# The token gate in one bank and the last group of heads normalised whole

## The chip, the core and the metric

One core of a Trainium2 chip runs the whole program. Its engines work from queues of their own and wait for each other by semaphores: TensorE (PE, matrix products into the eight PSUM banks), VectorE (DVE), ScalarE (ACT), GpSimd (POOL), and SyncE (SP), which here only issues transfers to the 16 DMA engines. The metric is the device time of one execution in microseconds. A profile is one execution taken by the hardware profiler; its span goes from the first to the last instruction.

## The reference

Two attention blocks over the same 2048 tokens of 512 channels, 32 heads of 16, mixed by a gate for each token:

```python
x = A_x
g = _sigmoid((x * gate_w).sum(-1, keepdims=True))
a = _A_ref(x, A_wqkv, A_wo)            # softmax attention
b = _B_ref(x, B_wqkv, B_w_phi, B_wo)   # linear attention with softmax features
return g * a + (1 - g) * b

# _A_ref, a head at a time
p = _softmax((q @ k.T) * Dh ** -0.5)
o = p @ v                              # then all heads @ wo
# _B_ref
phi_q = concat(softmax(q @ w_phi), softmax(-q @ w_phi)); phi_k the same of k
o = (phi_q @ (phi_k.T @ v)) / (phi_q @ sum(phi_k) + 1e-6)
```

Branch A costs most: 32 heads times 2048 x 2048 scores, each of which needs an exponential.

## The kernel before

**Packs.** Branch A is cut into 512 packs. A pack is 4 heads x 128 keys x 512 queries: four score products, one for each 32-row strip of the array (L963), written to four PSUM banks, each 128 x 512. Sixteen packs (all keys) make a group, a set of four heads for one block of 512 queries; there are 32 groups, numbered 0 to 31, eight for each block of queries (`qc`). A pair of groups (even, odd) shares the queries q0 to q15.

**Two ways to an exponential.** ACT takes the scores of most packs in turns of three and two blocks, writing ET (L1011). For the packs that the table `AWAY` names, one entry of five bits for each group, DVE does it instead: `_vector_bits` makes four products and evicts each bank as integers that stand for a power of two (L903, tile va, tag b), and `_vector_terms` adds three shifts to them (L919, tile vp, tag t), two packs at a time where a group has two. The value products (L1077) read ET, va and vp as weights of V (or vc, a scaled copy of V) in four 32-column strips of one bank, adding up a group's numerators and, in a row of ones, its denominators. Where PE would idle, products with zeros (L1084, L984) fill in.

**The plan.** The kernel first makes a list of operations (`Plan.op`), each with an engine, a cost, a due position `prio` counted in packs and an earliest position `rel`. `Plan.order` then simulates the five queues with those costs and takes for each engine the operation that is ready and due first. What comes out is a fixed order for each engine's queue; on the chip each queue runs strictly in that order. `SHIFT` adds an offset in packs to all operations with a tag: p12 is the value product of pack 12, b and t are the bits and terms of DVE packs, x their products, q10 the projection and the transfers of the queries of groups 20 and 21, g the normalisation of a group, gate the gate, n, o, h parts of branch B, y an output block. A PE bank is given to a job when its first product is placed, and given back by the job's last eviction.

**Queries.** `_proj_q` projects the queries of a pair of groups, evicts them (L675, qs) and SP spreads them with eight small transfers to qT (L677). Fifteen lists (q1 to q15) come this way.

**Normalising.** When a group's sums stand, DVE transposes the bank in 32 x 32 blocks into T1 (L1129), multiplies the denominators with 1 + exp(-gate) (L1136, tile gh), takes the reciprocal (L1138) and scales (L1140). For an odd group SP then spreads the pair with 16 small transfers (L1148, tile `turned`) and transposes by DMA into onTA (L1363). The last pair is done by other means, without DMA: group 30 is normalised alone, and group 31 by `_norm_last`, in two halves of 256 columns one after the other, each with transpose (L1107), den (L1111), rec (L1113), mul (L1114) and a transpose back into onTA (L1117).

**Output.** `_out` multiplies onTA with the output weights (L1457), four products `pr` for each tile of 128 tokens, on top of branch B's four (L1411). Of the last block's four tiles (`tt` 0 to 3) the products of the last pair, pr = 3, are the last of all; tt 1 and 3 are evicted by DVE (L1464, with a part put aside earlier by L1452), tt 0 and 2 by ACT (L1468). Each tile's store of 128 KB follows (L1473), tt 2 from ACT's queue, the rest from SP's.

**The gate.** `_gate` copies the gate weights to 128 equal columns (gwb, L728), multiplies them with the tokens in four banks of 512 tokens (L736), and DVE transposes each bank (L741) into the room of onTA, so that every strip of 32 partitions holds every token's sum. Then gate_z (L747) writes minus and plus the sums to gh, gate_exp (L752, on ACT) and gate_h (L754) make 1 + exp of both; gate_b (L757, L761) makes ghb for branch B. gh is needed first by the normalisation of group 1.

**Branch B** runs beside all this: weights fused (L1206 to L1229), projections (L641), features with 16 exponentials on ACT (L1281), sums, and the numerators (L1385, L1393), with transposes by DMA on SP.

Of the kernel before, what the change touches and what calls it, by code (L numbers as in the profile page):

```python
# [6 lines left out]
ACT = mybir.ActivationFunctionType  # L7
ALU = mybir.AluOpType
AX = mybir.AxisListType

P = 128
# [4 lines left out]
QCH = 512  # L16
# [360 lines left out]
class _Kernel:  # L377
# [42 lines left out]
    def _memory(self, ctx):  # L420
# [57 lines left out]
        self.gwb = self.bq[:, 0, QCH:2 * QCH].rearrange("p (c m) -> p c m", c=4)  # L478
# [246 lines left out]
    def _gate(self):  # L725
        op, NQC = self.plan.op, self.NQC
        b_gwb, last = self.b_gwb, []
        op("POOL", lambda e: e.tensor_copy(self.gwb, self.gw[:, :, None].to_broadcast([P, 4, P])), 1.0,  # L728
           reads=[self.b_gw], writes=[b_gwb], name="gwb", prio=15)
        z = self.onTA[:].rearrange("p s r j -> p (s r j)").bitcast(F32).rearrange("p (q b d) -> p q b d", q=NQC, d=32)  # L730
        for qc in range(NQC):
            job = Job()

            def mm(e, qc=qc, job=job):
                for c in range(4):
                    ins = e.matmul(self._bank(job), self.gwb[:, c, :], self.xT[:, c, QCH * qc:QCH * qc + QCH],  # L736
                                   start=(c == 0), stop=(c == 3))
                return ins
            m = op("PE", mm, 4 * self.c_pe(512), reads=[self.b_xT[qc], b_gwb], name="gate", prio=self.GATE + qc, rel=self.GATE - 6,
                   acquire=job)  # L740
            last.append(op("DVE", lambda e, qc=qc, job=job: e.transpose(  # L741
                z[:, qc].rearrange("p b d -> p (b d)"), self._bank(job)), 0.74, deps=[m], name="gate_t", prio=self.GATE + qc,
                release=job))
        flat = self.gh[:].rearrange("p r q b -> p (r q b)")
        col = z[:, :, :, 0].rearrange("p q b -> p (q b)")
        for r, sign in ((0, -1.0), (1, 1.0)):
            last.append(op("DVE", lambda e, r=r, sign=sign: e.tensor_scalar(  # L747
                self.gh[:, r].rearrange("p q b -> p (q b)"), col, sign, None, op0=ALU.mult), 0.2,
                deps=last, name="gate_z", prio=22))
        for b in self.b_onTA[0] + self.b_onTA[1]:  # L750
            b.readers = last[-2:]
        a = op("ACT", lambda e: e.activation(flat, flat, ACT.Exp), 0.2, deps=last, name="gate_exp", prio=24)  # L752
        self.b_g = Buf()
        op("DVE", lambda e: e.tensor_scalar(flat, flat, 1.0, None, op0=ALU.add), 0.25, deps=[a], writes=[self.b_g],  # L754
           name="gate_h", prio=24)
# [9 lines left out]
    AWAY = (15, 3, 9, 7, 27, 30, 29, 28, 26, 14, 15, 31, 14, 15, 27, 15, 15, 31, 23, 22, 31, 27, 13, 30, 27, 23, 11, 29, 31, 31, 21, 31)  # L765

    SHIFT = (
        ("p12", 11.5), ("k5", 3.5), ("k4", -8.5), ("v1", -2.5), ("p30", 10.5), ("p6", 13), ("p13", 1), ("p22", 7),
        ("p15", -5), ("q1", 3), ("w0", -13.5), ("p18", 6), ("b1", -9.5), ("v2", -4.5), ("x1", 2), ("v4", 6), ("p21",
        8), ("p2", 1), ("k1", -3), ("p26", -1.5), ("k6", 2), ("b4", -2.5), ("p9", -2), ("p0", 4.5), ("b42", 0.5),  # L770
        ("x4", -7.5), ("b20", -4), ("b55", 2.5), ("p40", 4), ("b52", -6.5), ("g1", 10), ("p36", 2), ("p38", 7),
        ("x33", -0.5), ("p31", 8), ("d0", -3.5), ("p34", -0.5), ("p32", -6.5), ("p39", 1), ("v9", 7), ("b68", -8.5),
        ("b65", -10.5), ("e2", -3.5), ("p62", -8), ("p54", -2), ("p47", -4), ("p59", -0.5), ("x77", 6), ("b87", 4),
        ("x65", 5.5), ("t84", -7.5), ("t65", 0.5), ("p75", -3), ("p70", 0.5), ("x68", -6), ("p72", 4.5), ("b93",
        6.5), ("x55", 11), ("b77", 5.5), ("b90", 7.5), ("a0", -1.5), ("p89", 1), ("p79", -0.5), ("g4", 9), ("x90",
        10), ("b97", 11.5), ("p92", 5), ("p94", 6.5), ("p104", 10.5), ("e5", -1.5), ("g5", 1.5), ("x103", -3),
        ("t90", 12), ("p98", -7.5), ("e4", -6), ("g6", 12), ("q5", 1.5), ("p124", -6), ("x138", -4), ("x122", 5),
        ("p140", -1.5), ("p126", -10.5), ("g7", 2), ("p127", -10), ("p121", 6.5), ("x141", -12), ("p116", -0.5),
        ("p137", -13.5), ("t125", -9), ("p113", -2), ("b132", -2.5), ("b125", -8.5), ("b138", -8), ("a4", -9),
        ("p136", -12), ("x109", 11), ("b154", 8.5), ("e8", 6), ("p112", 5.5), ("g8", 1), ("p152", 11), ("e11",  # L780
        -10.5), ("p157", -3), ("p149", -13.5), ("p158", -8), ("t154", -5), ("b170", 6), ("p155", 8.5), ("t148", 1),
        ("e9", 6), ("p147", -0.5), ("p144", 2.5), ("b167", 3), ("p171", 2.5), ("p172", 10), ("p159", 8), ("p168",
        8.5), ("p163", -7.5), ("p162", 0.5), ("a8", 9), ("x177", 11.5), ("p192", -11.5), ("p194", 2.5), ("p188",
        -2), ("g11", 1.5), ("e13", -1.5), ("p190", -8), ("x199", 10.5), ("p181", 8), ("b199", -4.5), ("p184", 11.5),
        ("p195", -2.5), ("b196", -5.5), ("d12", -13.5), ("p219", 4), ("x209", -13), ("p207", -8), ("p210", -8),
        ("p204", -8.5), ("t209", 11), ("p203", 3), ("p232", 12.5), ("p233", 8), ("f0", -5.5), ("b241", 8.5),
        ("x234", 3.5), ("t225", 12), ("a12", 14), ("p254", 3.5), ("p240", -14), ("b260", -1), ("p245", -11.5),
        ("p242", -13), ("b234", -12.5), ("p236", -8), ("b263", -11), ("g14", 2), ("p251", 12.5), ("b257", 8), ("h0",
        -8), ("t257", -11), ("t241", 2), ("b279", -3), ("x260", 13.5), ("p256", 3.5), ("p255", 8), ("p268", 6),
        ("p246", -0.5), ("p264", 2), ("p270", -3.5), ("p258", -1.5), ("p274", 5), ("p284", 2), ("g16", -11.5),  # L790
        ("x257", 6), ("b301", -8.5), ("p277", 9.5), ("p286", 3), ("p275", -11.5), ("p272", -2), ("t279", 10),
        ("b289", 7.5), ("b285", -0.5), ("p287", 14), ("p291", -5.5), ("b311", 3), ("p307", 2.5), ("p296", 1.5),
        ("p303", 2), ("p294", -4), ("b324", -10.5), ("p315", 8), ("p306", -12), ("t289", -5.5), ("x311", 8),
        ("p300", 10.5), ("p302", 14), ("x289", -4), ("o0", -8), ("p304", 8), ("x292", 8), ("p297", 5), ("p293", 2),
        ("b327", -6), ("h5", -10.5), ("n5", -9), ("x317", -3), ("o3", 3), ("p318", -4), ("n4", -9), ("p332", -4),
        ("p323", 2), ("p331", 4.5), ("q11", 0.5), ("b333", 13.5), ("p338", -9.5), ("p341", -1), ("x349", 14),
        ("h10", -7), ("p380", -10), ("p371", 6.5), ("p363", 6.5), ("p376", 12.5), ("o4", -8), ("o5", -3), ("p377",
        -1), ("b372", -13.5), ("h8", -4.5), ("x372", 8.5), ("o6", -11.5), ("h9", 10.5), ("p367", -0.5), ("p374",
        -1), ("p373", 2), ("x359", -9), ("g21", -1.5), ("p366", -6), ("x381", -4), ("b381", 1.5), ("x362", -2.5),
        ("p386", -1), ("p396", 0.5), ("b397", 5.5), ("n9", -4.5), ("b417", 13.5), ("f3", -8), ("b413", 2), ("b404",  # L800
        6), ("p414", -1.5), ("x385", 0.5), ("p411", -2), ("p409", 1.5), ("p392", 3.5), ("p400", 8), ("p416", -5.5),
        ("g25", -9), ("p419", -2.5), ("g24", -11.5), ("p421", -0.5), ("b420", 2.5), ("x413", -0.5), ("y384", -6),
        ("o8", -1), ("p403", -1), ("p405", -4.5), ("b433", 2), ("b439", 8), ("p423", -4.5), ("p436", -6.5), ("p438",
        2), ("o10", 1.5), ("h14", 10.5), ("t442", -11), ("p432", -10), ("x439", 0.5), ("o11", 3), ("p435", -0.5),
        ("h12", -6), ("g26", -8), ("x445", -13), ("p444", -1), ("g27", 4), ("p448", 7), ("n12", -13.5), ("b471",
        -2), ("x449", -1), ("p456", -6.5), ("q15", -11.5), ("p459", 1.5), ("b461", 6), ("t449", -0.5), ("x452", -5),
        ("t455", 12), ("p464", -0.5), ("p476", -9.5), ("p467", 2), ("t481", 14), ("p478", -13), ("p470", -7.5),
        ("p482", -7), ("b493", -6), ("p483", 3.5), ("p485", 13), ("x487", -5), ("t493", -0.5), ("o15", 2.5),
        ("p496", 9), ("p495", 5), ("t497", -0.5), ("g30", -1.5), ("p505", -2.5), ("x506", -8), ("x509", -0.5),
        ("p508", -8), ("g31", -5.5), ("p501", -1.5), ("p511", 0.5), ("b506", -2), ("v3", -9), ("t7", 1.5), ("p8",  # L810
        12.5), ("e1", -1), ("v8", 6.5), ("p41", -3), ("x52", -6), ("p50", 3.5), ("p64", -8), ("p82", 14), ("d4",
# [707 lines left out]
```

## Time and profile before

| what | us |
|---|---|
| median of 3 runs | 760.48 (759.04, 760.48, 760.72) |
| the profiled execution's own time | 759.64 |
| its span | 757.8 |
| ACT: first exponential starts, last one ends | 8.48, 748.63 |
| DVE: last term (L919) ends | 749.24 |
| granted TensorE clock, mean | 0.999 |
| DMA, mean | 29 GB/s |

The page gives each engine's busy time over the span, and then a view in 40 slices; ACT and DVE have the digit 9 in all slices but the first four and the last. A line of a group of instructions reads: source line, engine, operation, output<-input, shape, count, then total busy time and the mean of one, then how long the engine had been idle just before them and for whom it had waited. A line of the timeline reads: start, length, engine, line, operation, count, and in brackets the idle time before it and its releaser; neighbours of one kind are merged. A line of the waits reads: who waited for whom, the total, how often, and the longest.

SP's queue over the part that the change touches first (timeline, SP):

```
18.27 0.65 SPq L535 DMA_DIRECT2D WoB<-in_B_wo_dram  x1
28.61 5.36 SPq L677 DMA_DIRECT2D qT<-qs  x8
74.16 11.21 SPq L1148 DMA_DIRECT2D turned<-T  x16
86.59 1.23 SPq L1363 DMA_TRANSPOSE onTA<-turned  x1
95.67 4.99 SPq L677 DMA_DIRECT2D qT<-qs  x8
```

### The profile page before, as it was taken

The numbers are of one execution on the slowest core, as the hardware profiler recorded it, in microseconds if no ns is written. First come the engines' busy times: TensorE is split into PE (matmuls) and PEld (weight loads), VectorE is DVE, ScalarE is ACT, GpSimd is POOL, SyncE is SP. The second block draws the span as 40 slices with busy tenths as digits, with TensorE's granted clock in tenths as the row PEclk, the third lists the DMA queues.
The fourth block names the chain that finished last, engine by engine and source line by source line (L and its number), as shares of the span: only waits on it lengthen the run. The fifth ranks groups of instructions, "written<-read, shape, count | busy, mean of one in ns | idle before, by whom it ended". The sixth has DMA issues, their size and how long they took to land.

```text
span 757.8 us, 16775 instructions
## 1 busy us (share of the span) xinstructions
PE 718.0 (95%) x7172; PEld 229.8 (30%) x7241; DVE 730.0 (96%) x1138; ACT 740.4 (98%) x646; POOL 8.1 (1%) x17
## 2 busy tenths in 40 slices
PE   8999999999999999999999999999999998999997
PEld 3334333342322232232222222223232222222222
DVE  6989899999999999999999999999999999999997
ACT  6999999999999999999999999999999999999995
POOL 3000000000000000000000000000000000000000
PEclk9999999999999999999999999999999999999999
DMA  9300100000010010000003101411103102301120
GB/s 212 130 2 1 15 8 10 14 7 16 2 16 8 8 16 8 6 11 7 18 9 63 23 12 25 71 29 23 29 29 65 21 16 35 78 13 25 12 26 29
DMA packets 88745, 21.68 MB, mean 29 GB/s; under 512 B 81632, under 2 KB 88160, under 8 KB 88672
## 3 DMA queue, kind: packets, MB, share of 16 engines
q1 hardware_dynamic: 86944, 20.10, 13.8%
q8 instruction: 56, 0.92, 0.5%
q10 hardware_dynamic: 1728, 0.52, 0.3%
q14 instruction: 17, 0.14, 0.1%
HBM read 4.21 MB, written 2.10 MB: 8 GB/s over the span
## 4 chain that ended last, share of the span: by engine, by line
ACT 64%; DVE 21%; PE 12%; DMA 1%; issue 1%; SPq 1%; DVEq 0%
ACT ET L1011 62%; DVE va L903 9%; DVE vp L919 6%; PE ps L963 5%; PE ps L1077 3%; ACT bq L1281 3%; PE ps L641 2%; DVE btree L1270 1%; DVE bq L1279 1%; PE ps L714 1%; DVE T L1129 1%; SPq L677 1%; DMA xT<-in_A_x_dram 1%; PE ps L984 1%; DVE V L720 1%
## 5 line engine op out<-in xcount | busy, mean ns | idle before, releaser
L1011 ACT ACTIVATE ET<-ps 128x1536 bf16<-128x1536 f32 x626 | 712.2, 1345 | 7.1 <-PE ps L963 6.2
L963 PE MATMUL ps<-qT,kT 32*128 32x512 bf16 x2048 | 312.1, 384 | 17.7 <-ACT ET L1011 8.5
L903 DVE TENSOR_SCALAR va<-ps 128x512 uint16<-128x512 f32 x484 | 314.4, 681 | 6.3 <-PE ps L963 4.9
L919 DVE TENSOR_SCALAR vp<-va 128x4096 uint16<-128x4096 uint16 (+1 forms) x204 | 221.6, 1097 | 0.2
L963 PEld LDWEIGHTS ps<-qT,kT 32*128 32x128 bf16 x2048 | 80.8, 91 | 263.0 <-ACT ET L1011 157.2
L1077 PE MATMUL ps<-ET,V 128*32 128x512 bf16 x1564 | 149.0, 386 | 0.3
L1077 PE MATMUL ps<-vp,vc 128*32 128x512 bf16 x968 | 84.5, 384 | 0.9 <-DVE vp L919 0.9
L1077 PEld LDWEIGHTS ps<-ET,V 128*32 128x32 bf16 x1564 | 39.3, 95 | 65.0 <-issue 51.0
L641 PE MATMUL ps<-WB,xT 128*128 128x512 bf16 x169 | 50.8, 383 | 4.4 <-issue 1.5
L1084 PE MATMUL ps<-kT,zero 128*32 128x512 bf16 x580 | 50.2, 385 | 0.0
L1077 PE MATMUL ps<-va,V 128*32 128x512 bf16 x484 | 47.8, 385 | 0.0
L1077 PE MATMUL ps<-vp,V 128*32 128x512 bf16 x484 | 46.2, 384 | 0.7 <-DVE vp L919 0.6
L641 PE MATMUL ps<-xT,WA 128*128 128x512 bf16 (+1 forms) x107 | 30.6, 373 | 3.6 <-issue 2.3
L1077 PEld LDWEIGHTS ps<-vp,vc 128*32 128x32 bf16 x968 | 21.9, 95 | 35.2 <-issue 18.0
L1281 ACT ACTIVATE bq<-bq 128x2048 bf16<-128x2048 bf16 x16 | 32.1, 2024 | 0.0
L1252 DVE CAST bq<-ps 128x512 bf16<-128x512 f32 x32 | 21.7, 683 | 2.9 <-PE ps L641 2.8
L1129 DVE STREAM_TRANSPOSE T<-ps 128x512 f32<-128x512 f32 x31 | 22.0, 709 | 0.6 <-PE ps L1077 0.3
L714 PE MATMUL ps<-WA,xT 128*128 128x128 bf16 x256 | 20.4, 220 | 0.5 <-DVE V L720 0.3
L1457 PE MATMUL ps<-WoA,onTA 128*128 128x512 bf16 x62 | 19.3, 382 | 1.0 <-DVE onTA L1117 0.9
L1279 DVE TENSOR_TENSOR bq<-bq,btree 128x2048 bf16<-128x2048 bf16 x16 | 19.4, 1214 | 0.0
L1084 PEld LDWEIGHTS ps<-kT,zero 128*32 128x32 bf16 x580 | 12.6, 94 | 22.1 <-issue 20.3
L641 PEld LDWEIGHTS ps<-WB,xT 128*128 128x128 bf16 x192 | 11.9, 97 | 23.9 <-issue 14.4
(87 smaller groups left out, 346.2 us busy)
## 6 DMA issues: line engine op xcount, KB each, us to landing
turned<-T SPq DMA_DIRECT2D x240, 8.0 KB, 1.8
qT<-qs SPq DMA_DIRECT2D x120, 16.0 KB, 1.8
WB<-in_B_wqkv_dram SPq DMA_DIRECT2D x1, 1536.0 KB, 7.4
out_dram<-WB SPq DMA_DIRECT2D x12, 128.0 KB, 1.9
WA<-in_A_wqkv_dram SPq DMA_DIRECT2D x3, 384.0 KB, 5.6
WoA<-in_A_wo_dram SPq DMA_DIRECT2D x1, 512.0 KB, 8.5
WoB<-in_B_wo_dram SPq DMA_DIRECT2D x1, 512.0 KB, 8.3
WA<-in_A_wqkv_dram ACTq DMA_DIRECT2D x3, 128.0 KB, 4.0
```

Source lines behind the costliest of these rows:

```text
L641: ins = e.matmul(self._bank(job)[:, 0:n], lhs(c), rhs(c), start=(c == 0), stop=(c == 3))
L714: ins = e.matmul(self._bank(job)[:, P * tt:P * tt + P], self.xT[:, c, QCH * j + TOK * tt:QCH * j + TOK * tt + TOK], self.WA[:, 2, c, P * c ...
L903: parts.append(op("DVE", lambda e, j=j, job=job: e.tensor_scalar(self.va[:, pair, side, j, :], self._bank(job), SCALE * LOG2E * 128.0, (12 ...
L919: self.plan.op("DVE", lambda e, k=k, shift=shift: e.tensor_scalar(flat(self.vp[:, k]), flat(self.va[:, pair]), float(shift), None, op0=ALU ...
L963: return e.matmul(out, self.kT[32 * i:32 * i + 32, cp, kt * TOK:(kt + 1) * TOK], self.qT[32 * i:32 * i + 32, s, :], start=True, stop=True, ...
L1011: o = plan.op("ACT", lambda e: e.activation(self.ET[:, a % NS:a % NS + n, :], self.ps[:, self._ring(a):self._ring(a) + n, :], ACT.Exp, sca ...
L1077: ins = e.matmul(self._bank(ot)[32 * i:32 * i + 32, :], V[:, v0:v0 + 32], tile(), start=(kt == 0), stop=(kt == self.NT - 1), tile_position ...
L1084: ins = e.matmul(self._bank(ot)[32 * i:32 * i + 32, :], self.zero[:], self.kT[:, 0, 0:QCH], start=False, stop=False, tile_position=(0, 32 ...
L1129: op("DVE", lambda e: e.transpose(T1[:, side].rearrange("p b s -> p (b s)"), src()), 0.635, deps=last, writes=[b_T1[side]], name="n_t1", p ...
L1252: [lambda e, b, k=k: e.tensor_copy(bq[:, k].rearrange("p (g s v) -> p g s v", g=8, s=2)[:, :, 0, :], b.rearrange("p (g v) -> p g v", g=8))],
L1279: run("b_sub", two(2048), lambda e, out=out, t=t: e.tensor_tensor(out, p, spread(t[:, :, 0], 32), ALU.subtract), at, [pos, tree[side]], [buf])
L1281: op("ACT", lambda e, side=side: e.activation(sides[side], sides[side], ACT.Exp, scale=1.0 - 2 * side), self.c_act(2048) + 0.04, reads=[bu ...
```

## The change

1. The gate's weights are copied to 32 columns. The four blocks of 512 tokens go to the four 32-column strips of one bank, 16 products of 32 columns. One transpose follows, then gate_z, gate_exp and gate_h on 128 x 32 values (each strip has its own 512 tokens). Sixteen transfers on SP spread the result to all strips of gh.
2. `_norm_last` is gone: group 31 is normalised by `_norm`, whole, as the branch `side == 1 and alone` has it, with one transpose back.
3. The products pr = 3 of the last four tiles get due positions of their own, in the order tt = 1, 0, 3, 2.
4. AWAY and SHIFT have new values: 121 bits in both AWAY tables; SHIFT has 708 entries for 679, 26 of them unchanged.

```diff
-        self.gwb = self.bq[:, 0, QCH:2 * QCH].rearrange("p (c m) -> p c m", c=4)
+        self.gwb = self.bq[:, 0, QCH:QCH + P].rearrange("p (c m) -> p c m", c=4)
...
     def _gate(self):
         op, NQC = self.plan.op, self.NQC
         b_gwb, last = self.b_gwb, []
-        op("POOL", lambda e: e.tensor_copy(self.gwb, self.gw[:, :, None].to_broadcast([P, 4, P])), 1.0,
+        op("POOL", lambda e: e.tensor_copy(self.gwb, self.gw[:, :, None].to_broadcast([P, 4, 32])), 0.3,
            reads=[self.b_gw], writes=[b_gwb], name="gwb", prio=15)
...
+        room = self.onTA[:].rearrange("p s r j -> p (s r j)").bitcast(F32)
+        z = room[:, 0:QCH].rearrange("p (b d) -> p b d", d=32)
+        g = room[:, QCH:QCH + 32].rearrange("p (r b) -> p r b", r=2)
+        job = Job()
+
+        def mm(e):
+            for c in range(4):
+                for qc in range(NQC):
+                    ins = e.matmul(self._bank(job)[32 * qc:32 * qc + 32, :], self.gwb[:, c, :],
+                                   self.xT[:, c, QCH * qc:QCH * qc + QCH], start=(c == 0), stop=(c == 3),
+                                   tile_position=(0, 32 * qc), skip_group_check=True)
+            return ins
+
+        m = op("PE", mm, 0.95, reads=self.b_xT + [b_gwb], name="gate", prio=self.GATE, rel=self.GATE - 6, kind="col",
+               acquire=job, array=0.853)
+        m.tiles = [0, 1, 2, 3] * 4
+        t = op("DVE", lambda e: e.transpose(z.rearrange("p b d -> p (b d)"), self._bank(job)), 0.74, deps=[m],
+               name="gate_t", prio=self.GATE + 1, release=job)
         for r, sign in ((0, -1.0), (1, 1.0)):
             last.append(op("DVE", lambda e, r=r, sign=sign: e.tensor_scalar(
-                self.gh[:, r].rearrange("p q b -> p (q b)"), col, sign, None, op0=ALU.mult), 0.2,
-                deps=last, name="gate_z", prio=22))
+                g[:, r], z[:, :, 0], sign, None, op0=ALU.mult), 0.1, deps=[t], name="gate_z", prio=self.GATE + 2))
+        both = g.rearrange("p r b -> p (r b)")
+        a = op("ACT", lambda e: e.activation(both, both, ACT.Exp), 0.12, deps=last, name="gate_exp", prio=self.GATE + 3)
+        a = op("DVE", lambda e: e.tensor_scalar(both, both, 1.0, None, op0=ALU.add), 0.1, deps=[a], name="gate_h",
+               prio=self.GATE + 4)
+        self.b_g = Buf()
+        parts = [lambda e, qc=qc, h=h: e.dma_start(self.gh[32 * h:32 * h + 32, :, qc, :], g[32 * qc:32 * qc + 32])
+                 for qc in range(NQC) for h in range(4)]
+        d = self.dma("SP", "gate", parts, cost=0.6 * len(parts), writes=[self.b_g], deps=[a], prio=self.GATE + 5, lat=1.6)
         for b in self.b_onTA[0] + self.b_onTA[1]:
-            b.readers = last[-2:]
...
+            b.readers = [d]
...
-    AWAY = (15, 3, 9, 7, 27, 30, 29, 28, 26, 14, 15, 31, 14, 15, 27, 15, 15, 31, 23, 22, 31, 27, 13, 30, 27, 23, 11, 29, 31, 31, 21, 31)
+    AWAY = (15, 5, 27, 9, 19, 31, 28, 28, 26, 27, 23, 27, 22, 30, 31, 22, 15, 15, 23, 7, 31, 23, 23, 7, 27, 31, 11, 27, 15, 31, 23, 31)
...
     SHIFT = (
-        ("p12", 11.5), ("k5", 3.5), ("k4", -8.5), ("v1", -2.5), ("p30", 10.5), ("p6", 13), ("p13", 1), ("p22", 7),
...
+        ("q10", -9.5), ("p316", -5), ("o2", -3.5), ("p317", 1.5), ("p313", 9), ("p310", 9), ("p309", -8), ("x324",
...
     def _norm_a(self, g, last):
         qc, g8 = divmod(g, 8)
-        if g == self.NPACK // self.NT - 1:
-            return self._norm_last(qc, lambda: self._bank(self.ot[g]), last, self.onTA[:, qc % 2, g8 // 2, :], 16 * g + 17.0,
-                                   self.ot[g])
...
-    def _norm_last(self, qc, src, last, dst, due, job):
...
-                b_on = self.b_last[tt // 2] if final and pr == 3 else b_onTA[pr]
-                m = op("PE", mm, self.c_pe(512), reads=[b_on, self.b_WoA], deps=[m], name="outa",
-                       prio=due + (final and pr == 3), acquire=job if alone else None)
+                m = op("PE", mm, self.c_pe(512), reads=[b_onTA[pr], self.b_WoA], deps=[m], name="outa",
+                       prio=self.NPACK + 5 + (1, 0, 3, 2)[tt] if final and pr == 3 else due, acquire=job if alone else None)
```

## The prediction, made before the changed kernel was run

> **What bounds the kernel now.** I read the page's busy times first, then ScalarE's waits, then the timeline around each of its stalls and at the end.
>
> ```profile
> span 757.8 us, 16775 instructions
> PE 718.0 (95%) x7172; PEld 229.8 (30%) x7241; DVE 730.0 (96%) x1138; ACT 740.4 (98%) x646; POOL 8.1 (1%) x17
> ...
> ACT ET L1011 <- PE ps L963: 6.2, 5, 4.9
> ACT xT L1468 <- PE ps L1457: 5.2, 2, 4.3
> ACT L1011 <- issue: 2.3, 1, 2.3
> ```
>
> ScalarE (ACT) is the bound, VectorE (DVE) stands close behind. By the timeline ACT's first exponential starts at 8.48 and its last ends at 748.63: 740.15 us. Of the page's 740.4 busy us, 1.28 (table load) and 2 x 0.60 (last evictions) lie outside, so 737.9 are busy inside and 2.25 idle: 0.5 before 25.3, 0.19 at 189, 0.61 at 467, the rest in pieces under 0.13. After it stands a tail of 757.8 - 748.63 = 9.2 us. Nothing else can become shorter unless ACT gets less to do.
>
> ACT's work is what AWAY leaves it. Counting the bits, both tables send 121 packs of four 512-column score blocks to DVE, in 53 pairs and 15 singles, so the 626 exponentials stay. Only the spread over groups differs: groups 0-3 send 12 packs (11 before), 4-7 14 (15), 16-19 15 (16), 24-27 16 (15), 28-31 18 as before, though inside these group 28 has 4 (5) and group 30 has 4 (3).
>
> **The gate.** Old rows and the new ones put in their place:
>
> ```profile
> L1129 DVE STREAM_TRANSPOSE T<-ps 128x512 f32<-128x512 f32 x31 | 22.0, 709 | 0.6 <-PE ps L1077 0.3
> L741 DVE STREAM_TRANSPOSE onTA<-ps 128x512 f32<-128x512 f32 x4 | 2.8, 712 | 0.0
> L747 DVE TENSOR_SCALAR gh<-onTA 128x64 f32<-128x64 f32 x2 | 0.4, 212 | 0.0
> L752 ACT ACTIVATE gh<-gh 128x128 f32<-128x128 f32 x1 | 0.4, 363 | 0.0
> ```
>
> DVE loses 4 x 0.712 + 2 x 0.212 + 0.213 (gate_h) = 3.48 us and gets 1 x 0.712 + 2 x about 0.16 + about 0.17 = 1.2 (the small ones by the 128x16 product at 0.160): 2.3 us less. PE loses 16 full matmuls, and does 16 of a quarter's columns, four at a time, as the value products do (four in 0.21 us from start to start): 16 x 0.213 = 3.4 us become 0.85. On the path that is worth nothing: in 40 to 100 us DVE is busy 16.55, 18.51 and 18.64 of each 20 us, so 6.3 us stand idle there already, while ACT has no gap. Were that cover gone, it would be worth at most 2.3 us. On ACT gate_exp starts at 69.51 and the next exponential at 69.71, so it holds the engine 0.2 us; with 32 columns for 128 it holds it for something between 0 and 0.2: I take 0.05 off.
>
> What is added is 16 small transfers on SP's queue, behind the wait for gate_h. The nearest row is the spread of a pair of heads (turned, also 16 parts of 32 partitions): 10.3 to 11.4 us of SP for 16, each landing in 1.8. So SP is held some 11 us, 13 to the result. Queued behind it may be q1's eight parts (28.6 to 34.0, then 1.8 to land) and group 1's turned parts (from 74.2). Group 2, the first that needs q1, starts on ACT at about 55 (8.5 + 26 packs of 1.81, from 709 us of exponentials for 391 packs); 28.6 + 11 + 5.4 + 1.8 = 47 leaves 8 us. Group 1's normalisation waits for the gate today until 71.6 (its den product), so a gate spread by then costs nothing. Cost 0; without the cover, see the rivals. POOL's smaller gwb copy (0.61 us, now about a quarter) is off the path.
>
> **The last group.** Today, by the timeline:
>
> ```profile
> 749.79 0.45 DVE L1107 STREAM_TRANSPOSE T<-ps 128x256 f32<-128x256 f32 x1 [0.55 <-PE ps L1077]
> ...
> 752.09 0.68 DVE L1464 TENSOR_TENSOR xT<-xT,ps 128x512 bf16<-128x512 f32 x1
> ...
> 753.24 0.45 DVE L1117 STREAM_TRANSPOSE onTA<-T 128x256 bf16<-128x256 bf16 x1
> 753.74 0.60 PE L1457 MATMUL ps<-WoA,onTA 128*128 128x512 bf16 x2 [0.88 <-DVE onTA L1117]
> 754.17 0.69 DVE L1464 TENSOR_TENSOR xT<-xT,ps 128x512 bf16<-128x512 f32 x1 [0.48 <-PE ps L1457]
> 754.38 0.60 ACT L1468 ACTIVATE xT<-ps 128x512 bf16<-128x512 f32 x1 [0.89 <-PE ps L1457]
> 755.01 0.37 ACTq L1473 DMA_DIRECT2D out_dram<-xT  x1
> ```
>
> Two halves run one after the other, with an eviction pushed into the second. Whole, from 749.79: transpose 0.71, den 0.16, rec 0.245 and mul 0.417 (the rows of group 30, which is normalised alone: 128x16, 128x16, 128x256), back transpose 0.71 (no row; 256 columns take 0.446 there and 0.450 from PSUM, so 512 as the 0.709 row; at most 2 x 0.446), and 4 gaps of 0.03: ready at 752.15 instead of 753.69. PE has twelve matmuls of the first three products and of branch B to do from 749.67, 0.213 each, so it is free at 752.23. The four last products then start at 752.25, 752.46, 752.68 and 752.89 in the order tt = 1, 0, 3, 2. An eviction begins 0.43 after its matmul starts (753.74 to 754.17): DVE at 752.68 and, 0.61 later, 753.29; ACT at 752.89 and about 753.38. The last ends at 753.98 for 754.98: 1.0 us earlier. Against that the four stores of 128 KB now go out within 0.6 us. DMA moved the last two today at 326 GB/s in its fullest half microsecond, so four take 1.6 us from about 754.1, 0.15 later than the last alone would end. Gain **0.85**; ends 1.0 (no crowding) and 0.4 (the second pair of stores waits for the first).
>
> [...] The trace has 3.11 us for the ten and 2.24 for the five, so by its rows the gain stands; what a smaller one would make of the time is a rival below.
>
> **The order of everything else.** Nearly all of SHIFT is new, so each queue is rearranged. The largest stall inside the run has a plain cause:
>
> ```profile
> 458.94 5.88 SPq L677 DMA_DIRECT2D qT<-qs  x8
> ...
> 466.09 0.39 PE L963 MATMUL ps<-qT,kT 32*128 32x512 bf16 x1 [0.64 <-DMA qT<-qs]
> ...
> 467.71 1.45 ACT L1011 ACTIVATE ET<-ps 128x1536 bf16<-128x1536 f32 x1 [0.61 <-PE ps L963]
> ```
>
> The transfers of q10 stood on SP behind sixteen turned parts (446.17 to 457.6) and a transpose, landed at 466.04, and PE, which works in order, stood before the matmul that needs them. Of the fifteen lists that come this way it is the only one that PE waited for. The new SHIFT has ("q10", -9.5) where the old has none: 9.5 packs of about 1.45 us (740 / 512), 14 us earlier, which is before those turned parts. I take that 0.6 off. For all other stalls I take no change: the order can't be read from the table, and its bounds are -1.6 (all the other idle time gone) and +4.4 (below).
>
> **The sum.** Tail -0.85, late q10 -0.6, gate on ACT -0.05: **-1.5**. From the profiled execution's own time, 759.64 (span 757.8 and 1.84 around it), that is 758.1; from the median of the runs, 760.48, it is 759.0. The runs reach from 759.04 to 760.72, so the profiled one is an ordinary one; I put the forecast between the two, **758.6**, own range 757.6 to 759.6. The measurement tells some 0.2% (1.5 us) from no change, so faster means below 758.96.
>
> **The rivals.**
> *The stall only moves.* Another list of queries or another bank comes late by as much: the tail's gain alone, 758.6 + 0.6 = 759.2, no change. For it: the old order left 2.25 us of idle time in seven or more places. Against it: one stall of this size in 740 us.
> *The tail gives less.* The five whole instructions take as long as ten halves (3.11 us for 2.24), or the stores crowd: the gain is 0.4, its lower end, 759.05, no change. For it: no row has the whole back transpose. Against it: the 512-column transposes of 0.709 beside 0.450 for 256. [...]
> *All idle time goes.* Another -1.6: 757.0. For it: 121 packs in other places give DVE its early idle 6.3 us to use (12 packs in groups 0-3), and take a pack out of 16-19. Against it: 0.5 us lie in the start, where little moves.
> *DVE ends last (slower).* A pack costs DVE 4 x 0.605 for its bits and 3 x 0.6 for its terms (half of a pair's 1.2): 4.2 us; 4.4 by busy time ((314.4 + 221.6) / 121). Group 30 now has one more. From 690 to 749 DVE idles 0.8 us of 59, and today its last term ends at 749.24, 0.6 after the last exponential. If it can't get ahead in group 28, which has one less, the last values come up to 4.4 later: 758.6 + 4.4 = 763.0. Every microsecond counts once the last term ends more than 0.5 us after the last exponential. Against it: groups 28 to 31 together send 18 as before.
> *The spread delays queries.* If the gate's 16 transfers stand before q1 or q2 on SP and last 11 us, and the list comes late past its 8 us of room, PE stands as at 466 and ACT with it: 1 to 3 us, 760 to 762. Against it: SP is empty from 34 to 74.
>
> **Chances.** Forecast 0.43 (of it 0.37 faster, 0.06 none), all idle gone 0.10, stall moves 0.15 (none), tail less 0.05 (none), DVE last 0.13 (0.12 slower, 0.01 none), spread delays 0.14 (0.11 slower, 0.03 none). Faster 0.47, none 0.30, slower 0.23. The range goes from 757.2 to 762.5: below it lies half of the second rival, above it a part of the DVE's, under 0.2 together.
>
> **What would show it.** Last group: one 0.71 transpose, back transpose ending some 2.4 us after the first starts, last eviction 1 us nearer to that start. q10: no wait of PE on qT near 466, ACT's waits on PE under 1.7 us without the first. Gate: gate_exp with 32 columns, 16 transfers of about 0.65 us on SP, no idle time of ACT around them. DVE: first exponential at 8.5, last one ending at 748.0, DVE's last term within 0.6 of it. I am wrong if ACT's idle time inside grows past 2.3 us, or if the last term trails the last exponential by over a microsecond.

## The result, and the profile after

| | before | after |
|---|---|---|
| median (22 runs each, side by side) | 759.85 | 760.94 |
| range | 758.91 to 762.56 | 759.62 to 764.45 |
| ratio after / before, 95% interval | | 1.0017 [1.0009, 1.0025] |
| profiled execution: own time, span | 759.64, 757.8 | 759.62, 757.8 |
| first exponential starts, last one ends | 8.48, 748.63 | 8.71, 750.20 |
| ACT idle between the two | 2.25 | 3.35 |
| last group's first transpose to the end of the span | 8.01 | 7.06 |

The change made the kernel slower, by 1.1 us where 1.9 us of gain were forecast (758.6 from 760.48: 1.5 from the sum, the rest from a start between the profiled execution and the median of the first three runs). The loss is less than the 0.2% that the prediction called telling, but the interval lies clear of 1. The profiled execution of the changed kernel is the shortest of its 22. The page of the changed kernel (most lines of the code moved by +9: the exponential is L1020, the score product L972, the value product L1086, bits and terms L912 and L928):

```profile
span 757.8 us, 16834 instructions
...
PE 716.8 (95%) x7199; PEld 229.7 (30%) x7266; DVE 728.9 (96%) x1130; ACT 740.5 (98%) x646; POOL 7.8 (1%) x17
```

ACT's busy time is the same 740 us over the span. Its waits (who waited for whom, total us, times, longest):

```profile
ACT ET L1020 <- PE ps L972: 7.3, 6, 5.1
ACT xT L1445 <- PE ps L1435: 3.7, 1, 3.7
ACT L1020 <- issue: 2.3, 1, 2.3
```

The first wait row, without its longest (the start), was 1.3 us before and is 2.2 us now; the second, the tail's, fell from 5.2 to 3.7. So the end gained and the inside lost. The timeline shows where ACT lost, and then the tail:

```profile
434.33 3.71 ACT L1020 ACTIVATE ET<-ps 128x1536 bf16<-128x1536 f32 x3 [0.51 <-PE ps L972]
...
554.49 5.72 ACT L1020 ACTIVATE ET<-ps 128x1024 bf16<-128x1024 f32 x5 [0.72 <-PE ps L972]
...
750.74 0.72 DVE L1107 STREAM_TRANSPOSE T<-ps 128x512 f32<-128x512 f32 x1 [1.47 <-PE ps L1086]
...
752.45 0.71 DVE L1123 STREAM_TRANSPOSE onTA<-T 128x512 bf16<-128x512 bf16 x1
...
753.65 1.28 DVE L1441 TENSOR_TENSOR xT<-xT,ps 128x512 bf16<-128x512 f32 x2 [0.49 <-PE ps L1435]
753.86 1.08 ACT L1445 ACTIVATE xT<-ps 128x512 bf16<-128x512 f32 x2 [3.66 <-PE ps L1435]
```

Two stalls are new, 0.51 at 434 and 0.72 at 554; another of 0.45 stands at 732.44, and 0.61 at 467 is gone from this execution. The chain of work that ends in the stall at 434 says what is late (start, us, what):

```profile
428.99 0.48 DVE nb L1371
429.48 0.03 DVE va L912
429.50 3.52 DMA WT<-nb
...
433.12 0.49 DVE nb L1371
433.62 0.05 issue
433.66 0.30 PE ps L1363 x4
433.97 0.35 PE ps L972 x3
434.31 0.02 issue
434.33 2.37 ACT ET L1020 x2
```

A tile of branch B (nb, two buffers, even and odd tiles) is transposed by DMA in 3.52 us, where the plan reckons with 2.75 (cost 1.25 and `TURN` 1.5). It is tile 1. Tile 3 needs its buffer, so DVE stands, PE's numerator product waits for DVE, and the score product behind it on PE is what ACT misses. The table put them so close: the old SHIFT has no entry for n2 and n3, and tile 2, which uses the other buffer, stood between tiles 1 and 3, so that tile 3 was written at 446.88, 27 us after tile 1's transpose was issued. The new one has n2 at +9 and n3 at -10, so tile 3 follows tile 1 at once, 3.6 us after that issue, and tile 2 comes last. The stall at 554 begins in a like way: four output products (L1389) wait 1.09 us for another such transpose, with the score product behind them.

### The profile page after: what moved, and what is told of

It reads as the page before. It is cut to its first block, busy times and chain, and to the rows that moved or that the text cites. A ratio compares the mean times of both kernels' runs of the same rounds, so it can differ in the third digit from the quotient of the medians.

```text
span 757.8 us, 16834 instructions
## 1 busy us (share of the span) xinstructions
PE 716.8 (95%) x7199; PEld 229.7 (30%) x7266; DVE 728.9 (96%) x1130; ACT 740.5 (98%) x646; POOL 7.8 (1%) x17
## 4 chain that ended last, share of the span: by engine, by line
ACT 63%; DVE 17%; PE 17%; DMA 2%; issue 1%; DVEq 0%
ACT ET L1020 60%; DVE va L912 7%; PE ps L972 6%; PE ps L1086 5%; DVE vp L928 4%; ACT bq L1259 3%; PE ps L641 2%; DMA WT<-nb 1%; DVE nb L1371 1%; DVE T L1107 1%; DMA xT<-in_A_x_dram 1%; DVE btree L1248 1%; PE ps L714 1%; PE ps L1389 1%; PE ps L1093 1%
## 5 line engine op out<-in xcount | busy, mean ns | idle before, releaser
L1020 ACT ACTIVATE ET<-ps 128x1536 bf16<-128x1536 f32 x626 | 712.2, 1340 | 8.5 <-PE ps L972 7.3
L972 PE MATMUL ps<-qT,kT 32*128 32x512 bf16 x2048 | 315.1, 384 | 16.2 <-ACT ET L1020 9.6
L912 DVE TENSOR_SCALAR va<-ps 128x512 uint16<-128x512 f32 x484 | 315.2, 684 | 9.6 <-PE ps L972 7.8
L928 DVE TENSOR_SCALAR vp<-va 128x4096 uint16<-128x4096 uint16 (+1 forms) x204 | 221.9, 1099 | 2.0 <-PE ps L1086 1.5
L972 PEld LDWEIGHTS ps<-qT,kT 32*128 32x128 bf16 x2048 | 81.3, 91 | 266.5 <-ACT ET L1020 156.0
L1086 PE MATMUL ps<-ET,V 128*32 128x512 bf16 x1564 | 150.2, 386 | 0.3 <-DVE va L912 0.3
L1086 PE MATMUL ps<-vp,vc 128*32 128x512 bf16 x968 | 86.1, 384 | 0.5 <-DVE vp L928 0.4
L1086 PEld LDWEIGHTS ps<-ET,V 128*32 128x32 bf16 x1564 | 39.6, 94 | 66.3 <-issue 53.7
L1093 PE MATMUL ps<-kT,zero 128*32 128x512 bf16 x604 | 53.0, 385 | 0.0
L1086 PE MATMUL ps<-va,V 128*32 128x512 bf16 x484 | 47.4, 385 | 0.0
L1086 PE MATMUL ps<-vp,V 128*32 128x512 bf16 x484 | 47.0, 383 | 0.0
L1086 PEld LDWEIGHTS ps<-vp,vc 128*32 128x32 bf16 x968 | 22.3, 95 | 34.7 <-issue 20.7
L1389 PE MATMUL ps<-WoB,WT 128*128 128x512 bf16 x58 | 16.8, 382 | 2.6 <-DMA WT<-nb 1.1
```

The lines of the kernel that those rows point to most:

```text
L912: parts.append(op("DVE", lambda e, j=j, job=job: e.tensor_scalar(self.va[:, pair, side, j, :], self._bank(job), SCALE * LOG2E * 128.0, (12 ...
L928: self.plan.op("DVE", lambda e, k=k, shift=shift: e.tensor_scalar(flat(self.vp[:, k]), flat(self.va[:, pair]), float(shift), None, op0=ALU ...
L972: return e.matmul(out, self.kT[32 * i:32 * i + 32, cp, kt * TOK:(kt + 1) * TOK], self.qT[32 * i:32 * i + 32, s, :], start=True, stop=True, ...
L1020: o = plan.op("ACT", lambda e: e.activation(self.ET[:, a % NS:a % NS + n, :], self.ps[:, self._ring(a):self._ring(a) + n, :], ACT.Exp, sca ...
L1086: ins = e.matmul(self._bank(ot)[32 * i:32 * i + 32, :], V[:, v0:v0 + 32], tile(), start=(kt == 0), stop=(kt == self.NT - 1), tile_position ...
L1093: ins = e.matmul(self._bank(ot)[32 * i:32 * i + 32, :], self.zero[:], self.kT[:, 0, 0:QCH], start=False, stop=False, tile_position=(0, 32 ...
```

## The experiments

All were compared with runs of the kernel before on the same chip. Times are medians in us, with the range of the runs. The ratio is the one on record; it is not the quotient of the two medians, from which it differs by up to 0.0012.

| kernel | median | range | before | ratio [95%] |
|---|---|---|---|---|
| tail alone, old order | 758.54 | 758.12 to 759.42 | 759.81 | 0.9981 [0.9973, 0.9990] |
| gate alone, old order | 761.73 | 760.95 to 762.16 | 759.81 | 1.0025 [1.0014, 1.0035] |
| tail and gate, old order | 761.38 | 760.40 to 764.06 | 759.81 | 1.0028 [1.0017, 1.0039] |
| gate alone, old products kept | 759.32 | 758.52 to 759.96 | 759.70 | 0.9994 [0.9985, 1.0003] |
| changed, old tail | 761.47 | 760.37 to 766.38 | 759.70 | 1.0035 [1.0020, 1.0051] |
| changed, room for transfers | 758.95 | 757.98 to 761.35 | 759.70 | 0.9992 [0.9984, 1.0001] |
| the same, zero products near 550 | 758.72 | 758.26 to 759.34 | 759.46 | 0.9985 [0.9977, 0.9994] |
| changed, only those zero products | 760.42 | 759.59 to 761.13 | 759.46 | 1.0007 [0.9997, 1.0016] |
| tail, and q10's transfers earlier, old order | 758.01 | 757.65 to 758.69 | 759.70 | 0.9981 [0.9972, 0.9989] |
| the same with gate, old products kept | 758.35 | 757.78 to 759.16 | 759.46 | 0.9981 [0.9972, 0.9990] |

**The tail alone.** Old tables, old gate; `_norm_last` unused and the last products in the new order of due positions.

```diff
-        if g == self.NPACK // self.NT - 1:
-            return self._norm_last(...)
...
-                m = op(..., deps=[m], name="outa", prio=due + (final and pr == 3), ...)
+                m = op(..., deps=[m], name="outa",
+                       prio=self.NPACK + 5 + (1, 0, 3, 2)[tt] if final and pr == 3 else due, ...)
```

> The kernel before with its own tables and gate, only the last group normalised whole and the last four products in the new order; every other instruction stands in the old order. Theory A (the new order of the rest costs what the parts gain): 0.9 us under the kernel before, 758.9 for 759.85; in the profile the first transpose of the tail to the end of the span takes 7.1 us for 8.0. Theory B (the whole tail doesn't pay, since the four stores crowd): within 0.3 us of the kernel before.

758.54, 1.27 less than before. Its timeline at the end:

```profile
749.62 0.72 DVE L1129 STREAM_TRANSPOSE T<-ps 128x512 f32<-128x512 f32 x1 [0.55 <-PE ps L1077]
...
751.33 0.71 DVE L1145 STREAM_TRANSPOSE onTA<-T 128x512 bf16<-128x512 bf16 x1
752.53 1.28 DVE L1464 TENSOR_TENSOR xT<-xT,ps 128x512 bf16<-128x512 f32 x2 [0.48 <-PE ps L1457]
```

From the first transpose to the span's end (756.7) it is 7.08 us for 8.01: 0.93 gained, where 0.85 was forecast. The rest of the 1.27 is no more than the scatter of the runs. The tail does what was forecast.

**The gate alone.** The old order, with the new gate put in place of the old one afterwards: the first of the old gate's four jobs becomes the sixteen column products, the other twelve products and three transposes are dropped, and gate_z, gate_exp, gate_h and the sixteen transfers follow at once.

```diff
             p.order()
+            self._swap_gate()
...
+        gone = [x for x, _ in self.g_m[1:]] + self.g_t[1:]
+        for e in q:
+            q[e] = [o for o in q[e] if id(o) not in ids and o not in zs + [a, h]]
```

> The kernel before with its own tables and tail, only the gate changed: one bank, one transpose, 16 transfers behind the first queries on SP; the rest of the instructions keep the old order, three transposes fewer. Theory A: no change, within 0.4 us of 759.85, since DVE idles in that stretch and SP is empty. Theory C (the gate's spread or its wait on ScalarE costs time): 1 us or more above, with idle time of ScalarE between 28 and 75 us that the profile of before doesn't have.

761.73: 1.9 us slower. The gate was forecast at nothing. A table of stretches (from:to, length, busy time of PE, PEld, DVE, ACT and POOL, granted clock, DMA share, GB/s), first of this kernel, then of the kernel before:

```profile
58.00:61.00 3.00, 1.28 (x9) 0.38 (x9) 2.49 (x5) 3.00 (x4) 0.00 (x0) 1.00 0.00 0
61.00:64.00 3.00, 2.17 (x18) 0.91 (x18) 2.30 (x3) 3.00 (x4) 0.00 (x0) 0.74 0.00 0
64.00:67.00 3.00, 2.78 (x18) 1.14 (x16) 1.74 (x3) 2.25 (x2) 0.00 (x0) 0.50 0.00 0
67.00:70.00 3.00, 3.00 (x27) 1.75 (x24) 1.40 (x3) 2.36 (x2) 0.00 (x0) 0.62 0.02 5
```

```profile
58.00:61.00 3.00, 2.90 (x17) 0.85 (x15) 3.00 (x6) 3.00 (x4) 0.00 (x0) 1.00 0.00 0
...
64.00:67.00 3.00, 2.94 (x29) 1.42 (x28) 2.87 (x6) 3.00 (x3) 0.00 (x0) 1.00 0.02 5
```

Without the old gate's products PE is busy for 1.28 of the 3 us from 58 to 61, where it was 2.90. Then its granted clock goes to 0.50, for some seven us, and PE falls behind: ACT stalls by 0.92, 0.47, 0.42 and 0.17 us between 66 and 76. The mean clock of all seven runs is 0.994 to 0.996.

**Tail and gate in the old order.**

```diff
+ both edits above
```

> Both parts of the change in the old order, with the old tables. Theory A: 0.9 us under the kernel before, 758.9, and so about 2 us under the changed kernel, which has the same parts in the new order. Theories B and C: not under the kernel before.

761.38, where 758.9 was forecast. The loss is the gate's again, with the clock's fall (mean 0.991 to 0.996) and the same stalls between 66 and 76; beside the scatter of these seven runs the tail's gain doesn't show.

**The changed kernel in a second execution**, unchanged.

> The changed kernel as it is, a second profile. Theory A: ScalarE's idle time between its first and last exponential is again over 3 us, and its longest stalls end where a transfer lands late (transposes of nb at 433 and 551, lists of queries); their lengths differ from the first profile (0.51 and 0.72) with the landing times. If instead the same stalls stand with the same lengths and no transfer before them, the order on the engines alone makes them.

One run, 760.53, span 758.7. The two executions agree within 0.02 us until 430. Then this one stalls 0.88 at 434.70 and 0.59 at 462.60, where the first had 0.51 and none; the third, 0.70 at 555.68, is as long as before. The end of its chain into 462.60:

```profile
458.01 0.59 SPq L677
458.60 0.04 issue
458.64 2.40 DMA qT<-qs
461.03 0.05 issue
461.08 0.38 PE ps L972
461.46 0.76 PE ps L1086 x12
```

That is q10, which stands on SP behind the sixteen turned parts in this order too (442.12 to 453.34, then q10 from 453.39).

**The gate with the old products kept.** As the gate alone, but the twelve full gate products stay on PE. Their result isn't used.

```diff
-        gone = [x for x, _ in self.g_m[1:]] + self.g_t[1:]
+        gone = self.g_t[1:]
```

> The kernel before with the new gate in the old order (as in the run that took 761.73), but the twelve full gate products that the change removes stay on PE; their result is not used. Theory C (those products were the work that kept TensorE's granted clock up near 60 us): the granted clock stays at 1.0 from 58 to 70 us, the four ACT stalls between 66 and 76 us (2.0 us) go, and the time is that of before, 759.8 us (759.4 to 760.2). Rival S (the new gate's steps on DVE, ACT and SP cost it, its sixteen small transfers above all): 761.3 to 762.0 us, with the stalls still there.

759.32: the 1.9 us are gone. The stretches of this kernel:

```profile
58.00:61.00 3.00, 3.00 (x20) 0.83 (x16) 1.98 (x4) 3.00 (x4) 0.00 (x0) 1.00 0.00 0
...
64.00:67.00 3.00, 2.94 (x28) 1.35 (x26) 2.19 (x4) 3.00 (x4) 0.00 (x0) 1.00 0.03 5
```

Same DVE, ACT and SP steps as the gate alone; only PE's products differ. So in the old order the products that the change removes carried PE's clock (1.00 from 58 to 70 with them, down to 0.50 without), and the gate's sixteen transfers cost nothing that shows (0.9994 of the kernel before).

**The changed kernel with room for transfers.** Four nb buffers for two; on SP q10 first, then half of the turned parts, the nb transpose, and the other half; the output products of about 546 us behind the next score product.

```diff
-        rb, nb = self.rb[:, k], self.nb[:, k]
+        rb, nb = self.rb[:, k], self.nb[:, k] if tt < 2 else self.WB[:, tt, 2 * D:3 * D]
...
+                o.deps = [d for d in o.deps if d not in nbs] + ([nbs[t - 4]] if t >= 4 else [])
...
+        sp[i:i + 3] = [q10, first, nb, on]
...
+        pe[pe.index(out[0]):i + 1] = [o for o in pe[pe.index(out[0]):i + 1] if o not in out] + out
```

> The changed kernel, its order kept but for places where a transfer's result was awaited: branch B's normalised tiles get four buffers instead of two, q10's eight transfers and the tile transpose behind them are issued ahead of (and between) the sixteen turned parts, and the first output products after 546 us go behind the next score product. Theory T (the new order gives the results of transfers too little room): the ACT stalls near 434, 462 and 555 us go, 1.2 us in the first profile of the changed kernel and 2.2 us in the second, so about 759.3 us (758.7 to 759.9), against 760.9. Rival O (the order of the engines' own work, banks or the clock, makes the loss): the stalls only move, 760.5 to 761.3 us.

758.95, 2.0 us under the changed kernel, inside the range that theory T gave. The stalls at 434 and 462 are gone; ACT has none of 0.15 us or more between 14 and 556. The three parts of the edit were not tried one by one. The third stall is not gone: the profiled execution, one of the three longest of the eleven (760.24), has 2.33 us at 556, and the reason is seen in its stretches:

```profile
549.00:550.00 1.00, 0.94 (x11) 0.22 (x11) 1.00 (x3) 1.00 (x1) 0.00 (x0) 1.00 0.00 0
550.00:551.00 1.00, 0.01 (x2) 0.01 (x3) 1.00 (x2) 1.00 (x2) 0.00 (x0) 1.00 0.00 0
551.00:552.00 1.00, 1.00 (x14) 0.28 (x14) 1.00 (x2) 1.00 (x2) 0.00 (x0) 0.75 0.13 33
...
553.00:554.00 1.00, 1.00 (x4) 0.33 (x3) 1.00 (x2) 0.94 (x2) 0.00 (x0) 0.50 0.12 30
554.00:555.00 1.00, 1.00 (x3) 0.15 (x1) 0.34 (x1) 0.00 (x0) 0.00 (x0) 0.54 0.12 30
```

PE stands idle near 550 (now for DVE's terms, no longer for the transfer), and the clock falls to 0.50 for 3.4 us. The changed kernel has the same gap (1.09 us). In its first two profiles the clock held there, but 7 of its 22 runs have a mean clock of 0.996 to 0.998, and their median is 762.1, against 760.8 for the 14 at 1.0. That the clock falls in this very gap is seen in the profile of the changed kernel with the old tail (below), which has the same order here (a line of PE's timeline, one of the stretches, one of ACT's timeline):

```profile
551.72 1.45 PE L1420 MATMUL ps<-WoB,WT 128*128 128x512 bf16 x4 [1.06 <-DMA WT<-nb]
...
553.00:554.00 1.00, 1.00 (x10) 0.21 (x12) 0.00 (x0) 0.71 (x1) 0.00 (x0) 0.50 0.13 33
...
555.93 4.80 ACT L1020 ACTIVATE ET<-ps 128x1024 bf16<-128x1024 f32 x4 [2.23 <-PE ps L972]
```

The clock stands at 0.50 from 552.2 to 555.6, and ACT's stall is 2.23 us where the two profiles with the clock at 1.0 have 0.72 and 0.70.

**Zero products in that gap**, in the kernel above and in the changed kernel alone:

```diff
+        for k in range(4):
+            x = Op("PE", pad.fn, pad.cost, "pad", 0, -99, "col", 0.2)
+            pe.insert(i, x)
```

> The kernel that gives the transfers room (758.95), with four zero products (sixteen column tiles, 0.9 us) put on PE where it stood idle for 1.03 us near 550 us; in that run's profile the granted clock then fell to 0.50 for 3.3 us and ACT lost 2.33 us. Theory C: the idle stretch lets the clock fall, in some executions and not in others; with it filled the clock is 1.0 in every run, the median 758.6 us (758.2 to 759.0), and no run lies above 759.8 us (three of eleven did). Rival: what lowers the clock lies elsewhere; then the clock still falls in about three runs of ten and the median stays at 758.9 to 759.1 us.

> The changed kernel with the same four zero products ahead of the output products that wait 1.09 us for a transfer near 551 us, and nothing else. Theory C: the granted clock stays up there, so the scatter goes: no run above 761.5 us (of the changed kernel's 22 runs 7 were, six of them with a mean clock of 0.998 or less), the median 760.5 us (760.2 to 760.8), since the three stalls behind late transfers stay. Rival: the products delay what waits, 760.9 us or more, with the scatter as before.

758.72 and 760.42. With them no run of either kernel has a mean clock below 0.999 (3 of 11 and 7 of 22 without), and the highest are 759.34 (761.35 without) and 761.13 (764.45 without), as theory C has it. Between the two the transfers' room is worth 1.7 us. The products take some 0.5 off the changed kernel's median, which is not clear of the scatter, and all of its runs above 761.2 (9 of 22). Of the seven above 761.5 five, and not six, have a mean clock of 0.998 or less. The profile with the zero products alone has the stalls of transfers still: 0.60 at 435 and 0.72 at 463. The stall after 554 stays with the room too: 0.74 us in the first kernel, with the transfers out of the way, behind DVE's terms and the output products on PE. That part belongs to the rival, the order of the engines' own work.

**The changed kernel with the old tail.** `_norm_last` and the old positions of the last products back; all else as in the changed kernel.

```diff
+        if g == self.NPACK // self.NT - 1:
+            return self._norm_last(...)
...
-                       prio=self.NPACK + 5 + (1, 0, 3, 2)[tt] if final and pr == 3 else due, ...)
+                       prio=due + (final and pr == 3), ...)
```

> The changed kernel with the old tail (last group in two halves, last products in the old order); gate and order are the new ones. Theory: the tail is worth in the new order what it was in the old, 1.0 to 1.3 us, so 761.9 to 762.2 us against 760.9 for the changed kernel. Rival: behind the new order's later last products the tail gives little, 760.9 to 761.4 us.

761.47, 0.5 above the changed kernel, which is not clear of the scatter (5 of these 11 runs have a mean clock of 0.998 or less); from the first transpose (752.21) to the end (759.9) it is 7.69 us, 0.63 more than with the new tail. Both forecasts missed: the tail is worth 0.63 in the profile here, not 1.0 to 1.3. The whole version takes the same in both orders (7.08 and 7.06). It is the halves that end sooner in this one (7.69 for 8.01), behind the last eviction: from its end to the end of the span it is 2.5 us here and 2.8 in the kernel before. One profile of each doesn't say whether that is the order or scatter.

**The old order, tail and q10.** The last three of the sixteen turned parts go behind the nb transpose and q10.

```diff
+        first = self._cut(on, 13)
+        sp[i:i + 3] = [first, nb, q, on]
```

> The kernel before with the new tail alone (758.54), and on SP's queue the last three of the sixteen turned parts put behind q10's eight transfers. Theory T: the stall of ACT near 467 us (0.6 us in the profile of before) is a transfer that is issued late; it goes, and the time falls to 758.0 us (757.7 to 758.3). Rival: the time won there is lost at the next wait, 758.4 to 758.7 us.

758.01, the shortest median of all. SP's queue in it:

```profile
446.76 9.34 SPq L1148 DMA_DIRECT2D turned<-T  x13
456.14 1.27 SPq L1363 DMA_TRANSPOSE WT<-nb  x1
457.94 6.11 SPq L677 DMA_DIRECT2D qT<-qs  x8
464.10 1.93 SPq L1148 DMA_DIRECT2D turned<-T  x3
```

q10 goes out 0.7 us earlier than with the tail alone (458.64), and 1.3 us earlier against ACT's work, which starts 0.6 later in this execution. ACT's stall at 467 (0.50 there) is gone, and nothing stands in its place. How much that gives is less sure: the medians differ by 0.5, the ratios to the kernel before are both 0.9981.

**The same with the gate, old products kept.**

```diff
+            self._room(); self._swap_gate()
```

> The kernel before with the new tail, with q10's transfers ahead of the last three turned parts (758.01), and with the new gate beside the twelve old gate products, kept on PE without use (759.32 against 759.70 for the kernel before): if the two gains add up, 757.6 us (757.3 to 757.9). Rival: the gate's gain there is the stall near 467 us, which is gone already; 757.9 to 758.2 us.

758.35, above both forecasts, beside a slightly faster kernel before; the ratio is the same 0.9981. The gains don't add up. With the gate and the old products alone, the profile lacks the stall at 467 too, so it may be that this stall is what the gate's smaller work could win there, and that q10's place on SP wins it already.

## Why the prediction was wrong

- **The order of everything else (taken as no change): wrong, and the step that turned the sign.** I argued that an order can't be read from its table and put it at its middle, with +4.4 as its far end for another reason (DVE's terms). It cost 2.2 us: that is what returns when the changed kernel gets room for its transfers and its PE gap is filled (760.94 to 758.72). Of this, 1.7 to 2.0 return with the room alone: results of transfers were awaited too closely (3.52 us to landing ahead of the stall at 434, where the plan has 2.75; 2.40 for q10's last part in the second execution, where the median of such parts on the page of the first is 1.8). The stalls at 434 and 462 show 0.51 of it in one profile, 1.47 and 1.32 in two others; where the rest lies isn't shown. The remaining part is the clock near 550. One step might have been read from the table after all: n2 and n3 change places, and tile 3 shares tile 1's buffer. The form of the loss was among the rivals, as "the stall only moves", at 0.15 and with one stall moved. Here several came. The sign that the prediction named for its being wrong, ACT's idle time inside past 2.3 us, came true with 3.35.
- **Late q10 (-0.6): wrong.** The offset of -9.5 packs moved q10 by 6.5 us and not by 14, and the turned parts by 4.4, so q10 is still behind them:

```profile
441.76 10.66 SPq L1126 DMA_DIRECT2D turned<-T  x16
452.47 5.54 SPq L677 DMA_DIRECT2D qT<-qs  x8
```

Its users moved forward too: the product that waits for it starts at 461.08 in the second execution, and at 466.09 in the kernel before. So the list is in time in one execution and ACT stands for 0.59 in the next; this stall is part of the 2.2 us. That it is a matter of SP's order, the old order shows: with three parts moved the stall is gone, for a gain of 0.5 in the medians (758.54 to 758.01) and none in the ratios.

- **The gate (0): right for the changed kernel, wrong as an argument.** In it the first uses come as forecast, ACT has no stall of 0.15 us or more between 14 and 434, the transfers (10.27 us of SP) land before anybody waits for gh, and gate_exp holds ACT for 0.12 (0.20 before, so the -0.05 was right too). But "PE loses 16 full matmuls ... worth nothing" named no cover, because I looked for cover on DVE and ACT alone. In the old order the loss is 1.9 us, by PE's clock (0.50 for some seven us; with the old products kept it is 1.00 there, and the 1.9 us are gone). That the changed kernel keeps its clock there was luck, as far as the argument goes: in the new order other products fill the same stretch (PE is busy for 2.84 of the 3 us from 58 to 61) and the clock holds.
- **The last group (-0.85): right.** There is one transpose of 0.72, the back transpose ends 2.42 after the first starts (forecast 2.36), the last eviction ends 0.99 nearer to that start (forecast 1.0), and the end of the span 0.95; it is 0.93 in the old order, where the medians give 1.27. Against the old tail in the new order it is 0.63. "The tail gives less" by its own reason fell: the whole instructions took 2.28 us (0.72 + 0.18 + 0.25 + 0.42 + 0.71), near the 2.24 from the rows, and not the 3.11 of the ten instructions of the two halves.
- **DVE last, and the spread delays queries: fell.** The last term ends 0.93 us before the last exponential, where it ended 0.61 behind it in the kernel before, and ACT waits for no query before 430.
- Two small terms weren't seen: the first exponential starts 0.23 later, and ACT is busy for 0.24 us longer between its first and last exponential. The first is within what executions differ by (8.44 to 9.31 in the profiles of the old order alone). The cause of the second is open, as is that of the stall at 732, of 0.18 to 0.48 us in four profiles of the changed order and absent from two. The new order without the two code changes was not tried.

As a sum, for the first profile: +0.23 + 0.24 + 1.10 inside, -1.57 from the last exponential to the end. Of the 1.57 only 0.95 is the tail; the other 0.62 stands before its first transpose, where in the kernel before DVE's last term was still to come. That execution came out even, and the median is 1.3 us above it: the second execution stands for 1.47 at 434 and 462, where this one has 0.51, and 7 of the 22 runs have a mean clock of 0.996 to 0.998.

## What to carry to other kernels

Before taking work off an engine that is not the bound, look at how full that engine's next few microseconds are without it: products that nobody waits for may be what keeps PE's clock (here PE was busy for 1.28 of 3 us without them and the clock then fell to 0.50; with them it was busy for 3.00, and the clock stayed at 1.00). In an order that a planner writes out, list every consumer of a transfer with its room in the profile, and compare that room with the longest landing, not with the planned one (here 3.95 us and, in the kernel before, 4.3, for 2.75). Such stalls vary between executions (0.51 and 0.88 at 434), and so does the clock (1.00 around the gap near 550 in two profiles, 0.996 to 0.998 as the mean of 7 of 22 runs): one profile of each kernel says little, and the point where two executions of the same kernel part shows the place.

## What the runs showed of the hardware

The granted clock fell to 0.50 without any long pause of PE. With the gate alone it fell at about 62.4, after 3 us (58 to 61) with 1.28 busy, in which no idle stretch was longer than 0.65 us. With room for the transfers it fell at about 551.5, after one gap of 1.03 us (PE busy 1.59 of the 3 us from 548 to 551). It stayed there for some 7 us in the first and for 3.4 in the second. In the changed order one gap went both ways: around 1.09 and 1.06 us it held in the changed kernel's two profiles (busy 1.53 of the 3 us from 549 to 552, and 1.56 from 550 to 553), and around 1.06 us it fell with the old tail (1.56 from 549 to 552), for 3.4 us. So the falls came after stretches of 3 us in which PE was busy for 43% to 53%, and the clock held through two of 51% and 52%. What decides between the two isn't shown.

With sixteen products with zeros in the gap, all 22 runs of two kernels kept a mean clock of 0.999 or more; without them 3 of 11 and 7 of 22 were at 0.998 or less.

A DMA transpose of a 128 x 512 tile took 3.52 us and 3.95 us to land in the two places where an engine waited for it, while the median over all sixteen of the changed kernel is 2.5. In the kernel before the longest of sixteen took 4.3, and no engine waited for it.
